# Attention and two gated MLPs on one core: later scores from float32r parts, scaled first-batch queries, eight dummy matmuls

## The chip, the core and the metric

The kernel runs on one core of a Trainium2 chip. The metric is the device time of one execution in microseconds; a time given for a kernel is the median of its runs. TensorE (PE in the rows) multiplies and has a separate weight load (PEld); VectorE (DVE), ScalarE (ACT) and GpSimd (POOL) work elementwise; SyncE (SP) issues the DMAs.

## The reference

Attention with a threshold, then two gated MLPs on its output, all in float32:

```python
scores = scale * q @ k.T                       # 4 batches, 8 heads, 576 x 576, 64 wide
thresh = max(scores) - tau
attn   = softmax(where(scores >= thresh, scores, -1e9))
x      = attn @ v                              # -> 2304 tokens x 512
x      = x / rms(x) * g
x      = (silu(x @ wg) * (x @ wv)) @ wo        # 512 -> 1536 -> 512
x      = (silu(x @ wg2) * (x @ wv2)) @ wo2     # the same once more, no norm
```

The tolerance forbids plain bfloat16, so a float32 product is either done by float32 matmuls or from two float32r parts: a rounded copy (high) and the rest (low), with three products high·high, high·low, low·high.

## The kernel before

The 2304 tokens are worked in three blocks of 768 columns (b = 0, 1, 2). A block's attention covers one full batch and a third, or two parts of batches (`PHASES`); it is cut into 48 tiles of 128 query rows, 144 in all. The first block's 48 tiles are done ahead of everything by `fast`; the 96 later tiles are done by `tile_ops`, strewn between the MLP matmuls of the block before.

A tile's scores go through `QK` (TensorE, two halves of 288 keys in the two banks of a PSUM tile), `MAX` (VectorE, negated row maximum), `THR` (VectorE, threshold and exponent bias from the maximum and tau), `EXP` (ScalarE), `MASK` (VectorE, compare, multiply, sum), `REC` (two small GpSimd or VectorE operations and a reciprocal) and `normalise` (any of three engines, by `NORM_E`). In `fast` the result is transposed on TensorE (line 545, 550), copied out of PSUM (line 590 or 592, by `EV_E`) and multiplied by the values (line 566). In `tile_ops` it is split in two float16 parts (`HI_E`, `LO_E`: lines 461 to 470), transposed by DMA (line 475) and multiplied by the values in parts (lines 661, 664).

Queries and keys lie twice in SBUF, on partitions 0 to 63 and 64 to 127. So `QK` is, for each half j, a float32 matmul on 64 rows, on its own half of the array:

```python
k = slice(64 * j, 64 * j + 64)
nc.tensor.matmul(o[:, j], x[k, c0:c0 + w], x[k, S + j * HS:S + (j + 1) * HS], start=True, stop=True)
```

Of the 96 later tiles 88 hold rows of one head, 8 hold 64 rows of each of two heads, so there are 104 head parts with two such matmuls each. The profile records every float32 matmul as two.

The MLP matmuls are float32r on the whole array, 384 columns at a time (`dense`, line 876; in the last block most gate and value products are done with seven block products in place of eight, `gate_val7`, line 908). After 12 units of gate and value (f = 0 to 11) the output product is made in three pieces (`outp(0)`, `outp(1)`, `outp(2)`, after f = 4, 8 and 11), each from four hidden pieces h. A hidden piece is tanh on ScalarE (line 973), two VectorE operations (974, 985), a rounding copy on ScalarE (992) and a subtraction on VectorE or GpSimd (995); five of them have room (`r_h`).

The order on every engine is made by a planner (`Program.order`): each operation has an engine, an estimated cost, what it depends on and a priority (`OFF`, `OFFF`, the due times `ST` and `SU`), and of what is ready by the estimates the one of least priority goes next. Sets such as `V_E`, `W_E`, `H_E` say which operations go to VectorE and which to GpSimd. The engines then work strictly in that order and wait on semaphores.

Of the kernel before, what the change touches and what calls it, by code (L numbers as in the profile page):

```python
# [35 lines left out]
NU = 18  # L36
NTC = 12
# [58 lines left out]
S_E = (2, 0, 0)
RAWN, TN = 4, 1
ARENA = 17376
PLAIN = 1
GV = [m * NU + i for m in range(2) for i in [0, 1, 2, 3, 4, 7, 8, 9, 10, 13, 14, 15][PLAIN:]]  # L100
A_E = {3, 5, 8, 9, 10, 12, 13, 14, 15, 16, 17, 18, 20, 21, 22, 24, 26, 28, 29, 31, 32, 33, 35}
T_E = {0, 2, 3}

UP, FP, T0, DRAIN, ATT, LEAD, LEAD2, UL, RMS0, RMS1, CREL = 10071, 3560, 170023, -9692, 10886, 14, 9, 8063, -113807, -68190, 73599
OFF = {'MAX': 1748, 'EXP': 56850, 'THR': -2265, 'MASK': -95785, 'REC': 54966, 'NORM': 8371, 'HI': -109767, 'LO': 41933, 'LOL': 2327, 'DT': -94697, 'PV': 24084, 'PVO': 20003, 'PVA': 43347, 'SQ': -155048, 'SQA': -18773, 'SPV': 36844, 'CV': 57404, 'WL': -63278, 'WS2': -7942, 'WS': 9794, 'G': 22245, 'V': 3410, 'HH': 7267, 'YY': 23129, 'PUT': -4270}
OFFF = {'LV': 151718, 'QK': 353, 'MAX': 77575, 'THR': -110770, 'EXP': 9162, 'MASK': 33268, 'REC': -130346, 'NORM': 158475, 'TR': -48808, 'EV': -17099, 'PV': -54831, 'PVO': -31233, 'SQ': 1324, 'SQA': -215375}
EV_E = {0, 35, 5, 37, 8, 9, 41, 12, 46, 15, 49, 19, 51, 23, 27}
XO_E = {8, 17, 6}
# [121 lines left out]
BEGIN = dict(POOL=1400, DMA=1100)  # L230
# [11 lines left out]
def body(ctx: ExitStack, tc: tile.TileContext, qkv, tau, w1, rg, w2, outT):  # L242
# [43 lines left out]
    small = sb.tile([P, 30], F32, name="small")  # L286
# [16 lines left out]

    AR = sb.tile([P, ARENA], F32, name="arena", tag="arena")
# [7 lines left out]
    r_raw = Ring([take(2 * S) for _ in range(RAWN)])  # L312
# [12 lines left out]
    r_h = ring("h", 5, [P, 2, TW], F32R)  # L325
# [7 lines left out]
    late = []  # L333

    def arena2():
        if not late:
            late.append(sb.tile([P, ARENA], F32R, name="arena2", tag="arena"))
        return late[0]

    def TS(a, k):  # L340
        o = (4 * a + k) * 2 * HT
        return arena2()[:, o:o + 2 * HT].rearrange("p (i s) -> p i s", i=2)

    r_s = Ring([lambda i=i: arena2()[:, 16 * HT + i * 3584:16 * HT + (i + 1) * 3584].rearrange("p (a c) -> p a c", a=2) for i in range(3)])
# [4 lines left out]
    def retire():  # L349
        ops = {pg.wrote[k] for k in ("SQ",)} | {i for r in [r_raw, r_v, r_v3, r_e, r_ep, r_e16, r_ag, *r_tmp] for b in r.slots for i in b.ops}  # L350
# [33 lines left out]
    vs, raw = {}, {}  # L384
# [7 lines left out]
    def load(hd):  # L392
        _, c, b, q0, nq, _, _ = PAIRS[hd // 2]
        h = 2 * c + hd % 2
        t = r_raw.next()
# [198 lines left out]
    def tile_ops(n):  # L594
# [17 lines left out]
        for hd, *_ in parts:  # L612
            r += [("rawq", hd), ("rawk", hd)]
# [269 lines left out]
    def moe(b, between):  # L883
        for m in range(2):
# [146 lines left out]
            for f in range(NF):  # L1031
# [11 lines left out]
                elif f == 8:  # L1043
                    outp(1)
# [93 lines left out]
```

## Time and profile before

| | us |
|---|---|
| median of 3 runs | 1191.06 (1191.04 to 1192.66) |
| the profiled execution | 1193.02 |
| its span, first to last instruction | 1191.2 |
| TensorE busy in it | 1160.5 |
| VectorE, ScalarE, GpSimd busy | 840.1, 664.7, 513.2 |

TensorE's busy time counts the way of a matmul through the array, which overlaps the next one; so what a matmul costs in a row of them is read from the distance of their starts. In rows of the timeline the first number is a start, the second runs from the first start to the last end of the merged instructions. The first 18 us of the trace have no record of the granted clock, and the view of windows shows them as 1.00.

### The profile page before, as it was taken

The page shows a single profiled execution, that of the slowest core. Times are in us where ns is not written, and L with a number is a line of the kernel's source. Part 1 is how long each engine was busy: PE and PEld are TensorE (multiplying, and loading weights), DVE is VectorE, ACT ScalarE, POOL GpSimd, SP SyncE. Part 2 cuts the span into 40 slices and gives each one's busy share as a digit, 9 for nine tenths or more (in the row PEclk, how much of TensorE's full clock was granted, in tenths as well). Part 3 has the DMA queues.
Part 4 walks back from the last instruction along what each step waited for, and adds up shares of the span by engine and source line. Part 5 has one row for each costly group of instructions (what it writes and reads, how often), then busy time and mean ns, then how long its engine had stood idle before and what let it go on. Part 6 is the DMA issues. An engine that isn't in the chain of part 4 may idle for free.

```text
span 1191.2 us, 18894 instructions
## 1 busy us (share of the span) xinstructions
PE 1160.5 (97%) x7120; PEld 1024.6 (86%) x7120; DVE 840.1 (71%) x1533; ACT 664.7 (56%) x933; POOL 513.2 (43%) x582
## 2 busy tenths in 40 slices
PE   7998999999999999999999999999999999999998
PEld 4665888888888888888887888888999999999898
DVE  7998776778877777667667676755464867887743
ACT  5779867877887877434444343433332553454421
POOL 1222035656476566483635645432551512352221
PEclk9999989999999999999999999999999999999999
DMA  7323658998897998866683635444334212122111
GB/s 224 99 88 117 243 180 244 277 275 249 247 283 227 261 300 253 271 201 162 167 192 98 156 103 154 104 125 117 137 126 141 72 57 86 54 71 68 57 37 53
DMA packets 175291, 189.85 MB, mean 159 GB/s; under 512 B 143968, under 2 KB 147552, under 8 KB 164960
## 3 DMA queue, kind: packets, MB, share of 16 engines
q1 hardware_dynamic: 175200, 188.65, 54.5%
q8 instruction: 56, 0.92, 0.3%
q14 instruction: 35, 0.29, 0.1%
HBM read 119.93 MB, written 40.37 MB: 135 GB/s over the span
## 4 chain that ended last, share of the span: by engine, by line
PE 86%; DVE 6%; ACT 3%; DMA 2%; issue 1%; POOL 0%; SPq 0%; DVEq 0%; ACTq 0%
PE ps L876 58%; PE pb L908 10%; PE ps L609 5%; PE pt L661 4%; PE ps L908 2%; PE pt L664 2%; PE ps L506 2%; PE pt L566 1%; PE pt L545 1%; DMA arena<-arena 1%; ACT arena L592 1%; DMA arena<-in_qkv 1%; DVE h L995 1%; DMA w<-in_w 1%; DVE col L519 0%
## 5 line engine op out<-in xcount | busy, mean ns | idle before, releaser
L876 PE MATMUL ps<-XS,w 128*128 128x384 f32 x2400 | 445.3, 342 | 4.2 <-DVE th L974 3.0
L876 PEld LDWEIGHTS ps<-XS,w 128*128 128x128 f32 x2400 | 415.2, 190 | 33.7 <-issue 26.6
L876 PE MATMUL ps<-h,w 128*128 128x384 f32 x1728 | 319.0, 340 | 0.9 <-DVE h L995 0.6
L876 PEld LDWEIGHTS ps<-h,w 128*128 128x128 f32 x1728 | 300.1, 188 | 15.6 <-issue 13.0
L995 POOL TENSOR_TENSOR h<-th,h 128x768 fp32r<-128x768 f32 x37 | 71.8, 1941 | 138.6 <-ACT h L992 135.8
L626 DVE TENSOR_REDUCE col<-ps 128x1 f32<-128x576 f32 x96 | 72.3, 753 | 65.4 <-PE ps L609 65.1
L629 DVE SCALAR_TENSOR_TENSOR arena<-ps,col,arena 128x576 f32<-128x576 f32 x96 | 78.1, 814 | 43.4 <-ACT arena L628 42.9
L628 ACT ACTIVATE arena<-ps,col 128x576 f32<-128x576 f32 x96 | 70.9, 738 | 64.3 <-DVE col L627 55.9
L908 PE MATMUL pb<-arena 128*128 128x384 f32 x528 | 102.1, 339 | 3.1 <-DVE X L916 2.9
L908 PEld LDWEIGHTS pb<-arena 128*128 128x128 f32 x528 | 93.7, 191 | 3.8 <-DVE X L916 3.2
L775 ACT CAST w<-w 128x1024 fp32r<-128x1024 f32 x61 | 64.0, 1049 | 51.3 <-PE ps L876 43.2
L777 POOL TENSOR_TENSOR w<-w,w 128x1024 fp32r<-128x1024 f32 x27 | 65.8, 2437 | 52.7 <-ACT w L775 52.6
L992 ACT CAST h<-th 128x768 fp32r<-128x768 f32 x72 | 60.0, 833 | 46.7 <-DVE th L985 23.5
L1024 DVE SCALAR_TENSOR_TENSOR Y<-ps,Y 128x768 f32<-128x768 f32 x48 | 45.7, 954 | 47.3 <-PE ps L876 47.2
L973 ACT ACTIVATE th<-ps 128x768 f32<-128x768 f32 x48 | 38.9, 810 | 68.7 <-PE ps L876 67.2
L609 PE MATMUL ps<-arena 64*128 64x288 f32 (+1 forms) x416 | 73.4, 457 | 2.3 <-DVE arena L629 2.3
L469 POOL TENSOR_TENSOR arena<-arena 128x512 f16<-128x512 f32 x60 | 73.9, 1232 | 0.0
L974 DVE SCALAR_TENSOR_TENSOR th<-th,ps 128x768 f32<-128x768 f32 x48 | 45.6, 949 | 32.9 <-ACT th L973 32.6
L985 DVE SCALAR_TENSOR_TENSOR th<-th,ps 128x768 f32<-128x768 f32 x48 | 45.7, 951 | 32.7 <-PE ps L876 32.5
L450 ACT ACTIVATE arena<-arena,col 128x576 f32<-128x576 f32 x60 | 51.7, 864 | 22.6 <-DVE col L639 20.7
L918 ACT COPY X<-pb 128x384 f32<-128x384 f32 x66 | 31.3, 476 | 56.9 <-PE pb L908 56.7
L816 DVE SCALAR_TENSOR_TENSOR w<-w,t 128x1024 uint32<-128x1024 uint32 x36 | 50.0, 1388 | 7.7 <-ACT t L815 7.4
(146 smaller groups left out, 1781.9 us busy)
## 6 DMA issues: line engine op xcount, KB each, us to landing
w<-in_w SPq DMA_DIRECT2D x36, 1024.0 KB, 6.3
w<-kept SPq DMA_DIRECT2D x25, 1024.0 KB, 5.2
w<-kept SPq DMA_DIRECT2D x47, 512.0 KB, 3.7
kept<-w SPq DMA_DIRECT2D x19, 1024.0 KB, 5.4
kept<-w SPq DMA_DIRECT2D x30, 512.0 KB, 4.3
arena<-in_qkv SPq DMA_DIRECT2D x15, 576.0 KB, 4.3
arena<-in_qkv SPq DMA_DIRECT2D x41, 160.0 KB, 2.7
arena<-in_qkv SPq DMA_DIRECT2D x16, 288.0 KB, 3.3
```

Of the source, the lines that this page charges most:

```text
L450: op("ACT", 760, lambda: nc.scalar.activation(e, e, AF.Identity, bias=c[:, 4:5], scale=c[:, 3:4]), **k)
L469: op(en, 601 if eng == 2 else 1128, lambda: n1.tensor_tensor(h[:, 640:], e[:, :512], h[:, :512], ALU.subtract), lock=True, w=[("lo", n)], ...
L609: nc.tensor.matmul(o[:, j], x[k, c0:c0 + w], x[k, S + j * HS:S + (j + 1) * HS], start=True, stop=True)
L626: op("DVE", 670, lambda: nc.vector.tensor_reduce(c[:, 0:1], s2, AX.XY, ALU.max, negate=True), w=[*sk, ("mx", n)], bufs=[cb], p=T + F['MAX' ...
L628: op("ACT", 640, lambda: nc.scalar.activation(e2, s2, AF.Exp, bias=c[:, 2:3], scale=SCALE), r=[("thr", n)], w=[*sk, ("e", n)] + ek, bufs=[ ...
L629: op("DVE", 822, lambda: nc.vector.scalar_tensor_tensor(e2, s2, c[:, 1:2], e2, ALU.is_ge, ALU.mult, accum_out=c[:, 6:7]), r=[("thr", n)], ...
L775: op("ACT", 939, lambda: nc.scalar.copy(ws[:, 0], w), r=[("w32", n)], w=[("wh", n)], bufs=[b32, sbf], p=p, name=f"w_split{n}")
L777: op(en, 1142 if en == "DVE" else 2340, lambda: n1.tensor_tensor(ws[:, 1], w, f32(ws[:, 0]), ALU.subtract), lock=True, r=[("w32", n), ("wh ...
L876: nc.tensor.matmul(pt[:, j, :HT], w(i, a), x(i, b_)[:, j * HT:(j + 1) * HT], start=(i == 0 and a == 0 and b_ == 0), stop=(i == n - 1 and a ...
L908: nc.tensor.matmul(bank(), w()[:, a, col * 256 + i * P:][:, :P], xf(i, b_), start=first and i == 0 and a == 0 and b_ == 0, stop=i == 1 and ...
L992: op("ACT", 734, lambda: nc.scalar.copy(h[:, 0], tb.t), r=[("th", n)], w=[("h0", n)], bufs=[tb, hb], p=p + OFF['HH'], name=f"h{n}")
L995: op(eng, 878 if eng == "DVE" else 1795, lambda: n1.tensor_tensor(h[:, 1], tb.t, f32(h[:, 0]), ALU.subtract), lock=True, r=[("th", n), ("h ...
```

## The change

- **Scores of the 96 later tiles.** `split` makes, for each head of a later block, a tile of 128 rows: the rounded queries (64 rows) over the rest of the queries (64 rows), the rounded keys twice, and the rest of the keys twice. The rounding copies are ScalarE's or GpSimd's, the subtractions VectorE's or GpSimd's, by the new set `Q_E`. `QK` is then four float32r matmuls on 128 rows and 288 columns per head part, two that add up in each bank. A tile of two heads adds them up over eight, with columns of zeros for the other head's rows.
- **First block.** The queries are multiplied by 1/8 as they come in (one ScalarE and 16 GpSimd operations). The exponential takes the negated maximum itself as bias; `THR` is a GpSimd operation that only the mask waits for.
- **Start.** Eight float32 128x128x128 matmuls on the identity stand first on TensorE; the loads of tau and of the norm's weights are issued from ScalarE's queue in place of SyncE's.
- **Room.** The raw queries and keys get tiles of their own (five slots in the first block, two after it, with two for the parts); the arena is smaller; four hidden pieces have room in place of five, and `outp(0)` and `outp(1)` come after f = 3 and 7. The weights stand in DRAM as before and are read in the new order (`ROW`).
- **Tables.** Priorities, planner costs and all sets are new. In the first block 8 normalisations are VectorE's (16 before), 20 GpSimd's (8), 20 ScalarE's (24); VectorE has 16 copies of 512 columns (9), 9 of 128 (5), and 7 of the output copies (3). 36 weight pieces are kept with 16 stores of 1 MB and 26 of 0.5 MB (19 and 30).

```diff
-    r_raw = Ring([take(2 * S) for _ in range(RAWN)])
+    RA, RX = sb.tile([P, 4 * S], F32, name="ra", tag="ra"), sb.tile([P, 2 * XW], F32, name="rx", tag="rx")
+    slots = [RA[:, i * 2 * S:(i + 1) * 2 * S] for i in range(2)] + [RX[:, i * 2 * S:(i + 1) * 2 * S] for i in range(3)]
+    r_raw, r_raw2 = Ring(slots), Ring(slots[:2])
+    r_x = Ring([lambda i=i: again("rx", 2 * XW)[:, i * XW:(i + 1) * XW] for i in range(2)])
...
-    r_h = ring("h", 5, [P, 2, TW], F32R)
+    r_h = ring("h", 4, [P, 2, TW], F32R)
...
+            if hd == 0 and c0 == 0:
+                op("ACT", 180, lambda q=q: nc.scalar.activation(q, q, AF.Copy, scale=SCALE), w=keys, bufs=[tq], p=T_ - 20000, name=f"scale{hd}")
+            else:
+                op("POOL", 190 + (z - c0) * 8 // 10, lambda q=q: nc.gpsimd.tensor_scalar(q, q, SCALE, 1.0, ALU.mult, ALU.mult), w=keys, bufs=[tq], p=T_ + OFFF['QS'], name=f"scale{hd}")
...
+        for i, (key, a, z, o) in enumerate((("q", q0, q0 + nq, column(hd, q0)), ("k", S, 2 * S, S + 64))):
+            if 4 * hd + i in Q_E:
+                op("POOL", ..., lambda o=o, a=a, z=z: nc.gpsimd.tensor_scalar(xs()[:, o:o + z - a], ys[:, a:z], 1.0, 1.0, ALU.mult, ALU.mult), ...)
+            else:
+                op("ACT", ..., lambda o=o, a=a, z=z: nc.scalar.copy(xs()[:, o:o + z - a], ys[:, a:z]), ...)
+            en, n1 = ("DVE", nc.vector) if 4 * hd + 2 + i in Q_E else ("POOL", nc.gpsimd)
+            if i:
+                op(en, c, lambda n1=n1: n1.tensor_tensor(xs()[:, 2 * S + 64:], ys[:, S:], f32(xs()[:, S + 64:2 * S + 64]), ALU.subtract), ...)
+            else:
+                op(en, c, lambda n1=n1, o=o, a=a, z=z: n1.tensor_tensor(xs()[64:, o:o + z - a], ys[64:, a:z], f32(xs()[64:, o:o + z - a]), ALU.subtract), ...)
...
-            op("DVE", 130, lambda c=c, s=s: nc.vector.scalar_tensor_tensor(c[:, 1:3], s[:, 1, KC:KC + 2], c[:, 0:1], K2, ALU.mult, ALU.add), r=[("mx", n), "tau"], w=[("thr", n), *sk], ...)
-            op("ACT", 640, lambda c=c, s2=s2, e2=e2: nc.scalar.activation(e2, s2, AF.Exp, bias=c[:, 2:3], scale=SCALE), r=[("thr", n)], ...)
+            op("POOL", 270, lambda c=c: nc.gpsimd.tensor_scalar(c[:, 1:2], c[:, 0:1], K0[:, 0:1], ntau, ALU.mult, ALU.add), r=[("mx", n), "tau"], w=[("thr", n)], ...)
+            op("ACT", 640, lambda c=c, s2=s2, e2=e2: nc.scalar.activation(e2, s2, AF.Exp, bias=c[:, 0:1]), r=[("mx", n)], ...)
...
         def QK():
-            for hd, c0, w, m in parts:
-                x = raw[hd].t
-                o = s[m:m + w, :, :HS]
-                for j in range(2):
-                    k = slice(64 * j, 64 * j + 64)
-                    nc.tensor.matmul(o[:, j], x[k, c0:c0 + w], x[k, S + j * HS:S + (j + 1) * HS], start=True, stop=True)
+            for j in range(2):
+                for u, (hd, c0, w, m) in enumerate(heads):
+                    x = parts[hd].t()
+                    c = column(hd, c0) - m
+                    for i in range(2):
+                        k = S + 64 + (2 * i + j) * HS
+                        nc.tensor.matmul(s[:, j, :HS], x[:, c:c + P], x[:, k:k + HS], start=i + u == 0, stop=i == 1 and u == len(heads) - 1)
...
-                if f == 4:
+                if f == 3:
                     outp(0)
-                elif f == 8:
+                elif f == 7:
                     outp(1)
...
+    op("PE", 213 * WARM, warm, w=["PC"], p=-1e9, name="warm", cols=512 * WARM)
+    op("ACT", 60, lambda: nc.scalar.dma_start(taus, tau), w=["tau0"], p=-1e9, name="tau")
```

TensorE in the first MLP, at the end of the last gate and value unit ahead of `outp(0)`; `w` are weights, `XS` the inputs, `h` the hidden pieces, `ps_70` the scores' PSUM tile. Before:

```order
L876 MATMUL ps_65<-XS,w_103 128x384 x6
L609 MATMUL ps_70<-arena 128x288 x2
L876 MATMUL ps_65<-XS,w_103 128x384 x18
L876 MATMUL ps_66<-h_89,w_104 128x384 x6
L876 MATMUL ps_66<-h_90,w_104 128x384 x6
L876 MATMUL ps_66<-h_91,w_104 128x384 x6
L609 MATMUL ps_70<-arena 128x288 x2
L876 MATMUL ps_66<-h_92,w_104 128x384 x6
```

The same place after:

```order
L925 MATMUL ps_65<-XS,w_103 128x384 x18
L661 MATMUL ps_70<-rx_1190 128x288 x4
L925 MATMUL ps_65<-XS,w_103 128x384 x6
L925 MATMUL ps_66<-h_91,w_104 128x384 x6
L925 MATMUL ps_66<-h_92,w_104 128x384 x6
L925 MATMUL ps_66<-h_93,w_104 128x384 x6
L661 MATMUL ps_70<-rx_1190 128x288 x4
L925 MATMUL ps_65<-h_91,w_104 128x384 x6
L925 MATMUL ps_66<-h_94,w_104 128x384 x6
```

Each pair of matmuls of the scores has become four, at about the same places. The fourth hidden piece (`h_92` before, `h_94` after) is now that of the unit just ended, and another six matmuls on an older piece stand ahead of it.

VectorE at the start, from the third maximum on; `ps_65`, `ps_66`, `ps_70` are the three tiles of scores. Before:

```order
L520 SCALAR_TENSOR_TENSOR col<-ps_70,col,small 128x2
L520 SCALAR_TENSOR_TENSOR col<-ps_66,col,small 128x2
L519 TENSOR_REDUCE col<-ps_65 128x1
L522 SCALAR_TENSOR_TENSOR Y,col<-ps_70,col,Y 128x576
L520 SCALAR_TENSOR_TENSOR col<-ps_65,col,small 128x2
```

After:

```order
L573 SCALAR_TENSOR_TENSOR Y,col<-ps_70,col,Y 128x576
L570 TENSOR_REDUCE col<-ps_65 128x1
L573 SCALAR_TENSOR_TENSOR arena,col<-ps_66,col,arena 128x576
L570 TENSOR_REDUCE col<-ps_70 128x1
L573 SCALAR_TENSOR_TENSOR Y,col<-ps_65,col,Y 128x576
```

The thresholds (L520) are gone from VectorE, and masks and maxima alternate.

GpSimd after its constants (there is nothing between the constants and the first `REC` before), after the change:

```order
L1098 TENSOR_SCALAR small<-small 128x1
L1099 TENSOR_SCALAR small<-small 128x1
L431 TENSOR_SCALAR ra<-ra 128x448
L431 TENSOR_SCALAR ra<-ra 128x576
L431 TENSOR_SCALAR rx<-rx 128x192
L571 TENSOR_SCALAR col<-col,small 128x1
```

The first threshold (L571) stands behind the scaling of the queries of the second and of the third head (L431), which wait for their loads.

## Rows read from the trace of the kernel before

**Rows 1.** Windows by stage: us; busy of PE, PEld, DVE, ACT, POOL; PEclk; DMA; GB/s.

```profile
20.00:100.00 80.00, 75.62 (x750) 49.71 (x749) 74.69 (x199) 64.40 (x126) 19.14 (x55) 1.00 0.33 97
...
165.00:500.00 335.00, 334.31 (x1895) 286.38 (x1895) 251.42 (x423) 259.76 (x305) 205.48 (x252) 1.00 0.91 262
500.00:850.00 350.00, 347.26 (x2097) 301.89 (x2096) 224.11 (x496) 140.68 (x211) 165.97 (x179) 1.00 0.55 143
850.00:1191.20 341.20, 332.92 (x1905) 330.68 (x1903) 227.07 (x299) 137.26 (x195) 112.87 (x65) 0.99 0.24 81
```

**Rows 2.** Waits of TensorE: for whom, us in total, times, longest us.

```profile
PE ps L609 <- DVE arena L629: 2.3, 1, 2.3
PE pt L661 <- DMA arena<-arena: 1.1, 2, 0.7
...
PE ps L876 <- DVE h L995: 0.6, 1, 0.6
```

**Rows 3.** Timeline of TensorE around one later tile's scores (L609).

```profile
362.57 4.33 PE L876 MATMUL ps<-XS,w 128*128 128x384 f32 x24
366.82 0.76 PE L609 MATMUL ps<-arena 64*128 64x288 f32 x4
367.51 2.18 PE L876 MATMUL ps<-XS,w 128*128 128x384 f32 x11
```

**Rows 4.** The chain in order of time: start, us, what; float32r matmuls without a break.

```profile
966.34 6.24 PE pb L908 x36
```

**Rows 5.** The same timeline around a tile of two heads.

```profile
581.25 0.72 PE L609 MATMUL ps<-arena 64*64 64x288 f32 x8
581.90 1.32 PE L876 MATMUL ps<-h,w 128*128 128x384 f32 x6
```

**Rows 6.** The page's groups: count | busy us, mean ns | idle before it, releaser.

```profile
L609 PE MATMUL ps<-arena 64*128 64x288 f32 (+1 forms) x416 | 73.4, 457 | 2.3 <-DVE arena L629 2.3
```

**Rows 7.** Timeline of weight loads around the scores of rows 3.

```profile
366.39 0.19 PEld L876 LDWEIGHTS ps<-XS,w 128*128 128x128 f32 x1
...
367.51 0.30 PEld L876 LDWEIGHTS ps<-XS,w 128*128 128x128 f32 x2 [0.39 <-issue]
```

**Rows 8.** Groups by shape on VectorE, 0 to 117 us.

```profile
L520 DVE SCALAR_TENSOR_TENSOR col<-ps,col,small 128x2 f32<-128x2 f32 x48 | 9.8, 214 | 0.4
L590 DVE COPY arena<-pt 128x512 f32<-128x512 f32 x9 | 6.2, 684 | 1.1 <-PE pt L545 1.1
L448 DVE TENSOR_SCALAR arena<-arena,col 128x576 f32<-128x576 f32 x8 | 4.6, 574 | 0.0
...
L590 DVE COPY arena<-pt 128x128 f32<-128x128 f32 x5 | 1.4, 279 | 0.0
```

**Rows 9.** Groups by shape on GpSimd, 0 to 117 us.

```profile
L527 POOL TENSOR_SCALAR col<-col 128x2 f32<-128x2 f32 x20 | 4.8, 238 | 60.1 <-DVE Y L522 29.8 <-DVE arena L522 29.3 <-DVE col L531 1.0
...
L446 POOL TENSOR_SCALAR arena<-arena,col 128x576 f32<-128x576 f32 x4 | 3.3, 823 | 3.4 <-DVE col L520 1.4 <-PE ps L508 1.2 <-DVE col L531 0.8
```

**Rows 10.** Timeline of the start: the first mask, transposes on TensorE.

```profile
9.29 0.81 DVE L522 SCALAR_TENSOR_TENSOR Y<-ps,col,Y 128x576 f32<-128x576 f32 x1
...
14.13 1.97 PE L545 MATMUL pt<-ident,Y 128*128 128x128 f32 x8 [0.71 <-DVE Y L448]
```

**Rows 11.** Timeline of TensorE: transposes later in the first stage.

```profile
19.39 0.66 PE L545 MATMUL pt<-ident,arena 128*128 128x128 f32 x4
```

**Rows 12.** Groups by shape, whole span: work like the new splitting, and a hidden piece's last steps.

```profile
L469 POOL TENSOR_TENSOR arena<-arena 128x512 f16<-128x512 f32 x60 | 73.9, 1232 | 0.0
...
L995 POOL TENSOR_TENSOR h<-th,h 128x768 fp32r<-128x768 f32 x37 | 71.8, 1941 | 138.6 <-ACT h L992 135.8 <-DVE col L626 2.9
...
L992 ACT CAST h<-th 128x768 fp32r<-128x768 f32 x72 | 60.0, 833 | 46.7 <-DVE th L985 23.5 <-DVE th L942 23.0
...
L469 DVE TENSOR_TENSOR arena<-arena 128x512 f16<-128x512 f32 x36 | 24.9, 692 | 0.0
...
L461 ACT CAST arena<-arena 128x576 f16<-128x576 f32 x32 | 21.4, 667 | 19.7 <-DVE arena L448 15.7 <-issue 2.2 <-POOL X L677 1.7
```

More of the change, by code (lines that the diff above doesn't have):

```diff
@@ L96 @@
 S_E = (2, 0, 0)
-RAWN, TN = 4, 1
-ARENA = 17376
+TN = 1
+XW = 3 * S + 64
+WARM = 8
+ARENA = 12768
 PLAIN = 1
[L100 to L105, printed above, removed]
@@ L229 @@
 TICK = 10240 / 3
-BEGIN = dict(POOL=1400, DMA=1100)
+BEGIN = dict(POOL=1400, DMA=1100, PE=1500)
 LAT = {
@@ L285, in body @@
     make_identity(nc, ident)
-    small = sb.tile([P, 30], F32, name="small")
+    small = sb.tile([P, 31], F32, name="small")
+    ntau = small[:, 30:31]
     ones = small[:, 18:20]
@@ L302, in body, with again @@
     SS = RB = sb.tile([P, TW], F32, name="SS")
+    late = {}
+    def again(tag, n):
+        if tag not in late:
+            late[tag] = sb.tile([P, n], F32R, name=tag + "2", tag=tag)
+        return late[tag]
     AR = sb.tile([P, ARENA], F32, name="arena", tag="arena")
@@ L332, in body @@
     r_w = ring("w", 3, [P, 2, 1024], F32R)
[L333 to L338, printed above, removed]
     def TS(a, k):
-        o = (4 * a + k) * 2 * HT
-        return arena2()[:, o:o + 2 * HT].rearrange("p (i s) -> p i s", i=2)
-    r_s = Ring([lambda i=i: arena2()[:, 16 * HT + i * 3584:16 * HT + (i + 1) * 3584].rearrange("p (a c) -> p a c", a=2) for i in range(3)])
+        i, w = 4 * a + k, 2 * HT
+        t, o = (again("rx", 2 * XW), i) if i < 4 else (again("ra", 4 * S), i - 4) if i < 7 else (again("arena", ARENA)[:, 3 * 3584:], 0)
+        return t[:, o * w:(o + 1) * w].rearrange("p (i s) -> p i s", i=2)
+    r_s = Ring([lambda i=i: again("arena", ARENA)[:, i * 3584:(i + 1) * 3584].rearrange("p (a c) -> p a c", a=2) for i in range(3)])
     r_u = Ring([X.rearrange("p c s -> p (c s)")[:, i * 3 * HT:(i + 1) * 3 * HT].rearrange("p (u s) -> p u s", u=3) for i in range(2)])
@@ L382, in SK @@
         return [("SS", k) for k in range(a // 64, z // 64)]
-    vs, raw = {}, {}
+    vs, raw, parts, scales = {}, {}, {}, []
     def T_head(hd):
@@ L394, in load @@
         h = 2 * c + hd % 2
-        t = r_raw.next()
+        if hd == 2 * NFG:
+            for i in range(2):
+                r_raw2.slots[i].ops = list(r_raw.slots[i].ops)
+                r_x.slots[i].ops = [o for sl in r_raw.slots[2:] for o in sl.ops]
+        t = (r_raw if hd < 2 * NFG else r_raw2).next()
         raw[hd] = t
@@ L892, in gate_val7 @@
                 wb = wsp[n]
-                (b1, k1), (b2, k2), (b3, k3) = SETS[(next(x for x in (4, 8, 11) if x >= f) - f) % 2]
+                (b1, k1), (b2, k2), (b3, k3) = SETS[(next(x for x in (3, 7, 11) if x >= f) - f) % 2]
                 ub = r_u.next()
@@ L1040, in moe, with tau_consts, warm @@
                     tiles(2 * NTB)
[L1041 removed]
+                if f == 3:
                     outp(0)
[L1043 removed]
+                elif f == 7:
                     outp(1)
             outp(2)
[L1048 to L1049 removed]
+    def tau_consts():
+        nc.gpsimd.tensor_scalar(ntau, taus, -1.0, 1.0, ALU.mult, ALU.mult)
+        nc.gpsimd.tensor_scalar(K2[:, 0:1], taus, -1.0 / SCALE, 1.0, ALU.mult, ALU.mult)
+    def warm():
+        for _ in range(WARM):
+            nc.tensor.matmul(PC[:, :P], ident, ident, start=True, stop=True)
+    op("PE", 213 * WARM, warm, w=["PC"], p=-1e9, name="warm", cols=512 * WARM)
+    op("ACT", 60, lambda: nc.scalar.dma_start(taus, tau), w=["tau0"], p=-1e9, name="tau")
+    op("POOL", 130, lambda: tau_consts(), r=["tau0"], w=["tau"], rel=4000.0, p=-1e9, name="tau")
     for t, key in ((PA, "PA1"), (PB, "PB1"), (PD, "PD1")):
         op("ACT", 200, lambda t=t: nc.scalar.copy(t[:, 1, KC:KC + 2], K0), w=[key], p=0, name="K1")
[L1052 removed]
+    op("ACT", 60, lambda: nc.scalar.dma_start(rgs, rg), w=["rg"], p=-1e9, name="rg")
     done = [0]
```

90 lines of the change are left out of this document (59 added, 31 removed).

## The prediction

> **What bounds the kernel now.** I read the windows by stage first [rows 1]. From 165 us to the end TensorE is busy for 334.3 of 335, 347.3 of 350 and 332.9 of 341 us, while VectorE, ScalarE and GpSimd hold 60 to 78% in the densest of these stretches (251.4, 259.8 and 205.5 of 335). Then TensorE's waits [rows 2]: the longest behind 165 us are single ones of 2.3 us or less. So from 165 us on the time is TensorE's own work, and a matmul taken out there comes off the end, as long as the others keep up. Between 20 and 100 us it is otherwise: TensorE 75.6 and VectorE 74.7 of 80, ScalarE 64.4; no one engine sets the pace alone, and what one loses another may hold. Last I read starts on TensorE around the scores, since its busy time doesn't say what a group costs.
>
> **Scores of the later tiles, the large term.** A float32r matmul of 384 columns in an unbroken row takes 6.24/36 = 0.1733 us [rows 4]. In [rows 3] 24 such start at 362.57, so a 25th would start at 366.73; the scores start at 366.82, 0.09 later. The next MLP matmul starts at 367.51, 0.69 after the scores. Of the 11 that follow, the last ends at 369.69; with an end 0.34 us after its own start it starts at 369.35, 1.84 behind the first, where ten steps are 1.73: so 0.11 is lost once more. One tile of one head costs 0.09 + 0.69 + 0.11 = 0.89 us. A tile of two heads [rows 5] costs 0.65 from start to start; behind it six matmuls' last start is 0.98 after the first, where five steps are 0.87, 0.11 lost; with the same 0.09 ahead it is 0.85. The 416 records [rows 6] are 88 tiles at 4 and 8 at 8.
>
> After, a tile of one head is four float32r matmuls of 288 columns on the whole array, a tile of two heads eight. The trace has that type at 384 columns alone. At the granted clock (level 2.4 GHz, share 1.00 there) 384 columns stream in 0.160, so 0.0133 is added; for 288 I take 0.120 + 0.0133 = 0.133 us. The ends are 0.120 (nothing added) and 0.173 (no shorter than at 384). The weights have to be there in time: behind the scores, where nothing is loaded ahead, two loads take 0.30 together, where one takes 0.19 [rows 7], so they follow each other at 0.11, under the 0.120 of the stream. And I take no loss at the borders, since before and after stand matmuls of the same type and the same 128x128 tile, between which [rows 4] none shows. So 4 x 0.133 = 0.53 and 8 x 0.133 = 1.07 us. **Sum: 88 x (0.89 - 0.53) = 31.7 off, 8 x (1.07 - 0.85) = 1.8 on, 29.9 us off.** Ends: with 0.120, 88 x 0.41 = 36.1 off less 8 x 0.11 = 0.9, 35 off; with 0.173, 88 x 0.20 = 17.6 off, 8 x 0.53 = 4.3 on, 13 off.
>
> A rule of the Trainium skill speaks against this. Before, two 64-row matmuls run side by side on two halves of the array and the change gives that up. "TensorE: Matmul & The Clock Gate", Part 3, says moreover that a weight load overlaps a running matmul only where the row groups differ, and they don't between whole-array matmuls. By that rule [rows 4] would read 0.160 + 0.11 and more for each; it reads 0.173, so the trace doesn't agree where matmul follows matmul.
>
> **The splitting that pays for it.** 32 head loads each need two rounding copies and two subtractions: 48 copies on ScalarE, 16 on GpSimd, 25 subtractions on VectorE, 39 on GpSimd. By like rows [rows 12] a copy of 576 is 0.67 us on ScalarE, a subtraction of 512 is 0.69 on VectorE, 1.23 on GpSimd: at most 32 us on ScalarE, some 17 on VectorE, some 45 on GpSimd, all between about 120 and 870 us. From 165 to 500 the cover is what [rows 1] leaves free of 335 us, 84 on VectorE, 75 on ScalarE, 130 on GpSimd; half of the splitting fits in. What it can cost is order: a score's matmuls in front of the MLP's wait if the parts are late, and all of TensorE's queue behind them. I put 4 us, from 0 to 14 (14 is about half of the gain).
>
> **outp one unit sooner.** The fourth hidden piece must now be ready right after its own unit, at 12 more places (`outp(0)` and `outp(1)`, two MLPs, three blocks). Before, this holds at `outp(2)`, six places, and all waits for h by VectorE add up to 0.6 us [rows 2]: 0.1 each, 1 us for 12. The matmuls on older pieces that stand ahead, 24 x 0.173 = 4.2 us, cover copy and subtraction, 0.83 + 1.94 [rows 12]. If GpSimd is busy when the copy ends, another 1.94 isn't covered: 12 x 1.94 = 23 is the upper end, and 0 the lower.
>
> **The first stage.** VectorE loses 48 thresholds, 9.8 us, and 8 normalisations at 0.574, 4.6; it gains 7 copies at 0.684 and 8 small ones at about 0.28, 7.0 [rows 8]: 7.4 us less. ScalarE loses those copies and 4 normalisations. GpSimd gains 48 thresholds at about 0.24, 12 normalisations at 0.82 [rows 9], and the scaling, 16 operations between its small and its 576-column price: 11 + 10 + 4 to 13 on 19.1 of 80 us [rows 1], hidden. All 7.4 us come off only if VectorE alone sets the pace; TensorE, unchanged, has 4.4 of 80 us free, 5 on the whole stage. I take 4 off, from 0 to 8.
>
> **The start.** The first mask begins at 9.29 [rows 10]. The new exponential doesn't wait for tau, but the mask's threshold stands on GpSimd behind the scaling of the second and third head, whose loads come about then: no gain there. Eight transposes take 1.97 us at 14 us, four take 0.66 at 19 [rows 10, 11], so TensorE is slow up to there; eight dummies ahead of the first loads may end that sooner. 1 us off, from 1 on (first scores queue behind the dummies) to 2 off. The stretch from 100 to 165 us and the stores (5 MB fewer) I leave at nothing; 3 either way for the first.
>
> **Sum.** 1193.0 (the profiled execution; span 1191.2 and 1.8 around it) - 29.9 + 4 + 1 - 4 - 1 = 1163.1. The median lies 2.0 under that execution, so I predict **1161 us**.
>
> **Rivals**, all on the median.
> - *The others set the pace.* ScalarE and VectorE, three quarters full, and DMA (share 0.91 from 165 to 500) can't follow TensorE, and half of the gain stands as new waits: 15 back, 1176. For it: that stretch; against it: 0.7 us of DMA waits there at a time [rows 2], and only 55% DMA from 500 on.
> - *288 columns cost as 384.* The step is set by something other than the stream: 13 off instead of 30, 1178. Against it: the added 0.0133 is small beside the stream.
> - *Hidden pieces late.* 23 in place of 1 for outp: 1183.
> - *Loads not hidden, slower.* If two loads don't run under the shorter streams, a matmul takes 0.120 + 0.013 + 0.11 = 0.243, a tile 0.97 or 1.94: 88 x 0.08 + 8 x 1.09 = 16 on instead of 30 off, 1207. It decides above (88 x 0.89 + 8 x 0.85)/416 = 0.204 us a matmul. Against it stands [rows 4]; for it that 0.120 leaves but 0.01 over 0.11.
>
> **How the numbers follow.** Forecast 0.64 (its own range 1150 to 1170), others set the pace 0.17, as 384 columns 0.07, pieces late 0.05, loads not hidden 0.04; 0.03 for a new order that by several waits in TensorE's queue eats all the gain. The range goes from 1148 (35 off, first stage 8 off, and some of the 4 and 1 left) to 1180, which takes in the first two rivals. Faster by over 0.2% (2.4 us, about what a measurement here can tell from none) 0.91, within it 0.03, slower 0.06.
>
> **What would show it.** In the trace after: groups of four matmuls of scores about 0.53 from start to start of the next, with 0.173 straight ahead and behind; 0.24 would be the slower rival. TensorE without waits over 2 us from 165 us on, its instructions ending some 30 us sooner between 165 and 870; waits on the splitting's lines (471 to 479) or on h would show rivals one and three. The first stage's last maximum some 4 us sooner. A gain that lies mostly ahead of 165 us, or a loss behind 870, would make my reading wrong.

## The result and the profile after

The changed kernel took 1173.7 us (median of 4, 1172.6 to 1180.9), the kernel before beside it 1191.9 (1191.0 to 1196.4): a ratio of 0.985, interval 0.981 to 0.990. Two more sets of five runs gave 1172.9 (ratio 0.985, 0.982 to 0.987) and 1172.8 (0.984, 0.982 to 0.987). So it is faster by 18 to 21 us, inside the predicted 1148 to 1180, with about two thirds of the 30 forecast. The profiled executions tell the same: 1193.0 before, 1172.7 after, 20.3 less.

The page of the changed kernel: span, busy time of each engine, and the group of the later scores (busy, mean ns | idle before, releaser); they answer to the table of before and to [rows 6].

```profile
span 1170.9 us, 19172 instructions
...
PE 1138.1 (97%) x7136; PEld 1058.4 (90%) x7136; DVE 874.5 (75%) x1559; ACT 689.2 (59%) x973; POOL 588.3 (50%) x663
...
L661 PE MATMUL ps<-rx 128*128 128x288 f32 x416 | 71.9, 297 | 3.0 <-DVE arena L678 2.9
```

The windows of the changed kernel, columns as in [rows 1]:

```profile
20.00:100.00 80.00, 74.34 (x735) 48.45 (x729) 71.03 (x167) 55.58 (x107) 43.88 (x109) 1.00 0.30 92
...
165.00:500.00 335.00, 330.39 (x1954) 308.18 (x1953) 266.56 (x452) 271.00 (x332) 238.56 (x279) 1.00 0.89 250
500.00:850.00 350.00, 347.02 (x2165) 329.49 (x2164) 268.85 (x566) 167.50 (x247) 169.31 (x158) 1.00 0.56 143
850.00:1170.90 320.90, 313.92 (x1786) 312.94 (x1784) 203.03 (x267) 127.72 (x185) 108.90 (x59) 0.99 0.23 79
```

TensorE still fills the time from 165 us on, but no longer as tightly: 4.6 us idle from 165 to 500 in place of 0.7. The scores' group counts the same 416 records with nearly the same busy time as in [rows 6], 71.9 against 73.4: busy time shows nothing of the gain. The distances of the starts do. The timeline of TensorE after, around a tile of one head (L661 are scores, L925 MLP matmuls, L710 and L713 value products):

```profile
445.78 2.76 PE L925 MATMUL ps<-XS,w 128*128 128x384 f32 x15
448.38 0.69 PE L661 MATMUL ps<-rx 128*128 128x288 f32 x4
448.90 1.20 PE L925 MATMUL ps<-XS,w 128*128 128x384 f32 x6
452.38 1.62 PE L710 MATMUL pt<-arena 128*128 128x384 f16 x9 [2.27 <-DMA arena<-arena]
...
648.44 0.80 PE L661 MATMUL ps<-rx 128*128 128x288 f32 x4
649.09 4.33 PE L925 MATMUL ps<-XS,w 128*128 128x384 f32 x24
653.25 1.22 PE L661 MATMUL ps<-rx 128*128 128x288 f32 x8
654.31 4.33 PE L925 MATMUL ps<-XS,w 128*128 128x384 f32 x24
```

Fifteen steps of 0.1733 are 2.60, and the scores start 2.60 after the first: nothing is lost ahead. From there to the next MLP matmul it is 0.52 for four, 0.13 each; eight take 1.06. A tile of one head in [rows 3] cost 0.89. The group at 648.44 takes 0.65: it stands right behind a value product (L713), and there the first of the four takes 0.24 to the next one. The fourth row shows the other side, a new wait: the value product stood 2.27 us for its transposed parts.

The waits of TensorE between 165 and 850 us, columns as in [rows 2]:

```profile
PE pt L710 <- DMA arena<-arena: 3.4, 3, 2.3
PE ps L661 <- DVE arena L678: 2.9, 4, 1.4
PE ps L925 <- DVE th L1023: 0.7, 1, 0.7
```

To see where the 20.3 us went I count MLP matmuls (both kernels issue them in nearly the same order) and compare the start of the same one:

| stretch | before, us | after, us | difference | made of |
|---|---|---|---|---|
| start to first MLP matmul | 118.8 | 118.7 | -0.1 | |
| first to 200th | 51.3 | 52.4 | +1.1 | scores -1.7, rest +2.7 |
| 200th to 3250th | 694.9 | 675.7 | -19.2 | scores -26.1, waits +5.7, twelve matmuls of a later norm +1.3 |
| 3250th to the end | 326.3 | 324.2 | -2.1 | those twelve -1.3, waits -0.9 |

The scores' part is their own starts plus what the MLP matmuls beside them lost. This is one execution of each kernel. In two further profiles of the changed kernel (below) the stretches are 54.5 and 53.6, 673.1 and 675.2, 324.1 and 322.8 us: the large one holds within 3 us. TensorE's idle time from the 200th to the 3250th, 3.4 us before, is 7.6, 4.2 and 6.9 in the three. Up to 1.5 us of the -19.2 is the clock: from 639.6 to 643.0 us the kernel before ran at a granted clock of 0.50 (1.2 GHz), the changed one, in its first profile, nowhere in that stretch.

### The profile page after: what moved, and what is told of

Same layout as the page of the kernel before. It is cut to its first block, busy times and chain, and to the rows that moved or that the text cites. A ratio compares the mean times of both kernels' runs of the same rounds, so it can differ in the third digit from the quotient of the medians.

```text
span 1170.9 us, 19172 instructions
## 1 busy us (share of the span) xinstructions
PE 1138.1 (97%) x7136; PEld 1058.4 (90%) x7136; DVE 874.5 (75%) x1559; ACT 689.2 (59%) x973; POOL 588.3 (50%) x663
## 4 chain that ended last, share of the span: by engine, by line
PE 81%; DVE 6%; DMA 4%; ACT 4%; issue 2%; POOL 2%; SPq 0%; POOLq 0%; DVEq 0%; ACTq 0%
PE ps L925 53%; PE pb L957 12%; PE ps L661 4%; PE pt L710 4%; DMA arena<-arena 2%; PE ps L957 2%; DMA arena<-in_qkv 2%; PE pt L713 2%; PE pt L617 1%; PE ps L557 1%; PE pt L596 1%; ACT arena L643 1%; DVE w L865 1%; DVE col L570 1%; DVE Y L573 1%
## 5 line engine op out<-in xcount | busy, mean ns | idle before, releaser
L925 PE MATMUL ps<-XS,w 128*128 128x384 f32 x2400 | 438.9, 339 | 4.4 <-DVE XS L814 2.4
L925 PEld LDWEIGHTS ps<-XS,w 128*128 128x128 f32 x2400 | 415.4, 189 | 11.5 <-issue 4.3
L925 PE MATMUL ps<-h,w 128*128 128x384 f32 x1728 | 318.4, 338 | 2.8 <-DVE Y L1073 2.8
L925 PEld LDWEIGHTS ps<-h,w 128*128 128x128 f32 x1728 | 302.6, 188 | 6.0 <-DVE Y L1073 3.7
L1044 POOL TENSOR_TENSOR h<-th,h 128x768 fp32r<-128x768 f32 x33 | 64.5, 1955 | 103.3 <-ACT h L1041 103.3
L826 POOL TENSOR_TENSOR w<-w,w 128x1024 fp32r<-128x1024 f32 x30 | 74.4, 2480 | 83.2 <-ACT w L824 83.1
L957 PE MATMUL pb<-rx,arena 128*128 128x384 f32 x352 | 100.0, 338 | 0.0
L824 ACT CAST w<-w 128x1024 fp32r<-128x1024 f32 x60 | 62.9, 1049 | 44.6 <-PE ps L925 32.1
L661 PE MATMUL ps<-rx 128*128 128x288 f32 x416 | 71.9, 297 | 3.0 <-DVE arena L678 2.9
L661 PEld LDWEIGHTS ps<-rx 128*128 128x128 f32 x416 | 63.4, 188 | 7.0 <-DVE arena L678 4.6
L895 POOL TENSOR_TENSOR arena<-w,arena 128x768 fp32r<-128x768 f32 (+1 forms) x20 | 47.1, 2376 | 41.8 <-ACT arena L894 41.7
L957 PEld LDWEIGHTS pb<-rx,arena 128*128 128x128 f32 x352 | 64.5, 188 | 0.0
L1023 DVE SCALAR_TENSOR_TENSOR th<-th,ps 128x768 f32<-128x768 f32 x48 | 45.6, 950 | 22.3 <-ACT th L1022 22.0
L520 POOL TENSOR_TENSOR arena<-arena 128x512 f16<-128x512 f32 x52 | 61.2, 1178 | 0.0
```

The source lines that it names most:

```text
L520: op(en, 601 if eng == 2 else 1128, lambda: n1.tensor_tensor(h[:, 640:], e[:, :512], h[:, :512], ALU.subtract), lock=True, w=[("lo", n)], ...
L661: nc.tensor.matmul(s[:, j, :HS], x[:, c:c + P], x[:, k:k + HS], start=i + u == 0, stop=i == 1 and u == len(heads) - 1)
L824: op("ACT", 939, lambda: nc.scalar.copy(ws[:, 0], w), r=[("w32", n)], w=[("wh", n)], bufs=[b32, sbf], p=p, name=f"w_split{n}")
L826: op(en, 1142 if en == "DVE" else 2340, lambda: n1.tensor_tensor(ws[:, 1], w, f32(ws[:, 0]), ALU.subtract), lock=True, r=[("w32", n), ("wh ...
L925: nc.tensor.matmul(pt[:, j, :HT], w(i, a), x(i, b_)[:, j * HT:(j + 1) * HT], start=(i == 0 and a == 0 and b_ == 0), stop=(i == n - 1 and a ...
L957: nc.tensor.matmul(bank(), w()[:, a, col * 256 + i * P:][:, :P], xf(i, b_), start=first and i == 0 and a == 0 and b_ == 0, stop=i == 1 and ...
```

## Experiments

Ratios are to the kernel before on the same chip, from five rounds each. First the whole again, and what the largest part is worth by itself.

**The changed kernel again**, twice:

> The changed kernel once more, as the measure for the others of this call. Both theories: between 1172.6 and 1174.7 us, as in the first runs.

> The kernel after the change once more, as the measure for the two others of this call: 1172.8 us within 1.5, the first normalisation at 140 to 143 us.

Measured: 1172.9 and 1172.8. In their profiles the 200th MLP matmul starts at 173.8 and 173.0 (171.0 in the first one): a profile's single events move by 2 to 3 us between executions, the medians of the three sets by 0.9. Much of it is TensorE's clock: from 150 to 160 us the granted clock is 0.66 in these two and 0.83 in the first, so they spend more of it at the lower level (1.2 GHz). What that costs shows in the first profile: twelve MLP matmuls took 4.04 us at 132.4 us, mostly at the lower level, and 2.35 at 126.1, at the full clock.

**Scores by float32 again:**

```
- for each head part and half j: two float32r matmuls, 128 rows, x 288 columns
+ for each head part and half j: one float32 matmul on its 64 rows; split() not called; five raw slots
```

> The changed kernel with the later scores by float32 matmuls on 64 rows again, no splitting, all five raw slots used throughout; the planner orders it anew by the same tables. Theory 1 (the scores' matmuls give their whole 28 us, and what is missing of the forecast was lost elsewhere): slower than the changed kernel by 24 to 30 us, so 1197 to 1204, and slower than the kernel before; in the trace the later scores cost 0.89 us a tile again, and the first MLP matmul starts at 118 to 119 us as in both. Theory 2 (VectorE, ScalarE and GpSimd, loaded with the splitting, take back a part of the gain): slower by 10 to 20 us only, 1184 to 1194.

Measured: 1203.5 (1203.2 to 1205.7), ratio 1.011 (1.008 to 1.013): 30.6 above the changed kernel. Its timeline around a tile (L639 scores, L903 MLP matmuls) has the old pattern back:

```profile
379.66 2.28 PE L903 MATMUL ps<-h,w 128*128 128x384 f32 x12
381.88 0.76 PE L639 MATMUL ps<-ra 64*128 64x288 f32 x4
382.56 4.51 PE L903 MATMUL ps<-h,w 128*128 128x384 f32 x24
```

Scores at 2.22 where twelve steps are 2.08, and 0.68 to the next. By the starts some 27 of the 30.6 us are the scores' own; the rest is waits in this order (from the first to the 200th MLP matmul it takes 58.1 us, 3.6 of them idle ahead of scores). So this part carries the whole gain; the rest of the change is worth nothing, or less: this kernel is 11.5 us slower than the one before. How much of that comes from tables made for other costs stays open.

**What splitting costs:**

```
- n1.tensor_tensor(low, raw, high, subtract)   # both, for queries and for keys
+ (not issued; the scores' second halves read the high keys again)
```

> The changed kernel with the 64 subtractions of the splitting planned but not issued (25 on VectorE, 39 on GpSimd); the scores read the high parts in their place, so their values are not the reference's. Everything else stands in the same order. Theory 1: faster than the changed kernel by 3 to 6 us, about 1168, with TensorE's waits ahead of the scores and of the value matmuls between 165 and 870 us gone by half. Theory 2: faster by 8 us or more.

Measured: 1170.8 (1169.2 to 1174.7), 2.1 under the changed kernel measured beside it (1170.8 to 1175.7), less than either expected and hardly clear of the scatter: the ratios' intervals, 0.981 to 0.986 and 0.982 to 0.987, overlap. TensorE's waits ahead of scores and value products between the 200th and the 3250th MLP matmul sum to 2.6 us; in the three profiles of the changed kernel they are 6.5, 3.1 and 5.9, so that half of them went is not shown.

**The dummies:**

```
- for _ in range(WARM):
+ for _ in range(0):
```

> The changed kernel with the eight dummy matmuls planned but not issued. Theory 1 (they matter little, since TensorE falls back to the lower clock at 10.5 us): within 1 us of the changed kernel, 1172 to 1175; the first maximum 0 to 0.2 us sooner. Rival (the early clock counts): 1 to 3 us slower, with the first MLP matmul as much later.

Measured: 1172.7 (1170.6 to 1174.4): no difference. The timelines of TensorE show why, first with the dummies (L1103; L557 scores, L596 transposes), then without; between them two windows with the dummies, columns as in [rows 1]:

```profile
1.35 3.78 PE L1103 MATMUL pt<-ident 128*128 128x128 f32 x16 [1.35 <-POOL ident masks.py:199]
5.06 2.39 PE L557 MATMUL ps<-ra 64*128 64x288 f32 x8
...
8.51 0.76 PE L557 MATMUL ps<-ra 64*128 64x288 f32 x4 [1.06 <-POOL ra L431]
...
15.61 1.90 PE L596 MATMUL pt<-ident,Y 128*128 128x128 f32 x8
```

```profile
10.00:15.00 5.00, 4.23 (x16) 1.82 (x16) 4.97 (x12) 2.76 (x4) 2.67 (x9) 0.55 1.04 391
15.00:20.00 5.00, 4.98 (x43) 3.33 (x39) 4.89 (x13) 3.78 (x6) 2.80 (x7) 0.77 0.85 252
```

```profile
11.65 1.33 PE L557 MATMUL ps<-ra 64*128 64x288 f32 x4
...
15.85 1.85 PE L596 MATMUL pt<-ident,Y 128*128 128x128 f32 x8
```

With them the first scores start at 5.06 (4.43 without, 3.83 before), and eight transposes at 15.6 are as slow as ever (1.97 in [rows 10]). The dummies did reach the clock, for a moment: four records of scores take 0.76 us at 8.5 us where they take 1.33 without, and this trace's record of the granted clock reads 1.00 from 7.1 to 10.5 us. Then TensorE waited (1.06 us ahead of 8.51, 0.75 ahead of 10.02), and from 10.5 to 17.3 us the granted clock is 0.50 (1.2 GHz). In the second profile of the changed kernel four records take 1.33 us throughout: there the dummies did nothing.

Then the first stage, which I had at 4 us and which gave nothing. First theories: ScalarE's queue sets its end (theory 1), or VectorE's.

**Thresholds back on VectorE:**

```
- op("POOL", 270, ... nc.gpsimd.tensor_scalar(...))   # THR of the first block
+ op("POOL", 270, ... nc.vector.tensor_scalar(...))   # same place in the order
```

> The first block's 48 thresholds are issued by VectorE (as before the change) instead of GpSimd, at the same place in the order. Theory 1: the end of the first stage is set by ScalarE's queue (exponentials with the first weight units' conversions among them), so the first MLP matmul stays at 118.7 us within 1 and the total at 1172.9 within 1.5. Rival: VectorE's queue sets the pace of the first stage; then 48 instructions of 0.15 to 0.21 us each come back and the first MLP matmul and the total are 7 to 10 us later.

Measured: 1172.9 (1170.3 to 1176.2), no difference; the first MLP matmul at 120.1, 0.8 to 1.5 later than in the changed kernel's profiles. VectorE doesn't set the pace: 48 instructions, 12.7 us of its time in this trace, move the end by about 1.

**Conversions left out.** ScalarE is busy 18.0 of the 18 us from 100 to 118 in both kernels, with the first weight units' conversions among the exponentials.

```
- lambda: nc.scalar.activation(q, top, ...)               # three per unit
+ lambda: None if n < 2 else nc.scalar.activation(q, top, ...)
```

> The kernel before with ScalarE's conversions of the first two weight units not issued (the weights are wrong for it), which takes 7.4 us off ScalarE's queue around 97 to 121 us; all else in the same order. Theory 1: ScalarE's queue sets the end of the first stage, so the first MLP matmul, at 118.8 us before, comes 3 to 7 us sooner. Rival: the end is set by GpSimd or VectorE, or by the weights' transfers; then it moves by less than 1 us.

> The kernel after the change with ScalarE's conversions of the first two weight units not issued (the weights are wrong for it); all else in the same order. Theory 1: the first MLP matmul, at 118.7 us in after, comes 4 to 9 us sooner, and some 2 us sooner than in the kernel before with the same conversions left out: the scores of the first stage ended 2.2 us sooner in after, and ScalarE's queue had taken that back. Rival: it moves by less than 1 us, or both kernels move alike.

Measured: before 1189.8 (ratio 0.9986, 0.9969 to 1.0004), after 1172.6: neither moves by more than the runs can tell. The first MLP matmul came 1.4 us sooner in before (117.4) and 1.9 in after (116.8), out of 7.4 us taken away. Theory 1 as I put it falls, and what else holds the first MLP matmul at 118.7 in both kernels stays open. What was won was gone again by the 100th MLP matmul: 151.4 without the conversions, 151.6 with.

**A collision between 118 and 128 us.** The timelines of VectorE and GpSimd after (L826 is a weight's subtraction, L635 a sum of squares, L477 and L479 the first split):

```profile
122.62 1.53 DVE L477 TENSOR_TENSOR rx<-ra,rx 128x576 fp32r<-128x576 f32 x1
124.08 2.40 DVE L635 TENSOR_TENSOR SS<-SS,arena 128x64 f32<-128x64 f32 x1
...
122.03 1.50 POOL L479 TENSOR_TENSOR rx<-ra,rx 64x384 fp32r<-64x384 f32 x1 [5.36 <-ACT X L643]
123.97 2.42 POOL L826 TENSOR_TENSOR w<-w,w 128x1024 fp32r<-128x1024 f32 x1 [0.43 <-ACT w L824]
```

A sum of 64 columns takes 2.40 us beside GpSimd's subtraction; elsewhere 0.22. The Trainium skill ("SBUF — State Buffer", "Who interferes with whom") states that a VectorE instruction with two inputs in SBUF contends with a GpSimd instruction that reads SBUF; this pair agrees. Is it the cause?

```
- n1.tensor_tensor(...)                                      # rests of unit 1 and of the first pair's queries
+ (nc.vector if n == 1 else n1).tensor_tensor(...)           # likewise for the queries
```

> Between 118 and 150 us GpSimd works beside VectorE, and VectorE's small instructions there take 1.5 to 2.4 us where 0.2 to 0.3 are usual. Here weight unit 1's rests and the first pair's query rests are made by VectorE instead of GpSimd, at the same place in the order. Theory 1: the two engines collide there and that delays the first sum of squares; without it the 50th to 200th MLP matmul start 2 to 4 us sooner than after's, and the total is 1 to 3 us shorter than 1172.9. Rival: the long instructions there don't hold up the chain; the same milestones within 1 us and the total within 1 us, or later, as VectorE has more to do.

Measured: 1174.5 (1171.1 to 1179.7), none of the milestones sooner. The 64-column sum takes 0.22 again, and nothing comes of it.

**Transfers.** The first normalisation (L771, L722 before) started at 140.3 to 142.5 us in the changed kernel's profiles, at 139.0 before. In before, four raw loads went out between 100 and 110 us; in after they stand behind the second weight load, at 123.6 to 127.9, in full DMA engines.

```
- nc.sync.dma_start(t.t[:, c0:c1], qkv[b, h, :, c0:c1])
+ None if hd in (2 * NFG + 2, 2 * NFG + 3) else nc.sync.dma_start(...)   # first kernel
+ op("DMA", ..., rel=142000 if hd in (...) else 0)                       # second: not before then in the plan
```

> The four raw loads of the second later pair (queries and keys of two heads, 0.98 MB, issued at 123.6 to 127.9 us in after, where the DMA engines are busy 0.92 to 1.01 of the time from 120 to 140 us; in before they were issued between 100 and 110 us, at a DMA share of 0.39) are not issued, so that pair's scores come from the first pair's data and part of the output is not the reference's. All else is in the same order. Theory 3: full DMA engines hold VectorE's queue (its combination of the values waits for their load, and the first normalisation stands behind it), and these loads add 2.5 to 3 us there. Then the value load is 2 to 3 us sooner, the first normalisation starts at 137.5 to 139.5 us (140.1 to 143.1 in every run of the changed kernel with these loads there, 139.0 and 139.2 in the two of the kernel before), and the total is 1 to 3 us under after's of the same call. Rival: the queues of VectorE and ScalarE are full for other reasons, and the normalisation starts at 140 to 143 us all the same.

> The same four loads are released later, so that they stand in SyncE's queue behind the next weight load (issued at 138.4 us in after) and not ahead of two; on the other engines nothing moves but one pair of VectorE's instructions that changes places. Nothing is left out. Theory 3: as without those loads, the first normalisation starts at 137.5 to 139.5 us, and the total is 1 to 3 us under after's, since the second pair's scores are needed only after 160 us; this would then be the better kernel. Rival: it starts at 140 to 143 us as before, and the total is after's within 1 us, or above it by a wait of the second pair's scores for the later loads.

Measured: 1172.6 and 1173.5, the normalisation at 140.3 and 141.6. DMA's busy share from 125 to 130 us fell from 1.00 to 0.50 and 0.54. The value load that VectorE waits for landed at 138.8 in the first, as in the changed kernel (138.8 to 141.0), at 137.7 in the second. There the pair that changed places puts a weight's conversion (L865) behind the values' combination, and its subtraction then stands for ScalarE's rounding copy of that weight (L824):

```profile
140.45 1.23 DVE L826 TENSOR_TENSOR w<-w,w 128x1024 fp32r<-128x1024 f32 x1 [1.12 <-ACT w L824]
```

Theory 3 falls, and the second is no better kernel.

**Two brakes at once.** The rows left two: the timeline of VectorE without the conversions (L486 combines a head's values, L826 a weight's subtraction) has the first normalisation right behind a wait for a load,

```profile
138.57 0.49 DVE L486 TENSOR_TENSOR arena<-arena 128x320 f32<-128x320 f32 x1 [2.14 <-DMA arena<-in_qkv]
138.98 1.22 DVE L826 TENSOR_TENSOR w<-w,w 128x1024 fp32r<-128x1024 f32 x1
140.12 4.27 DVE L771 SCALAR_TENSOR_TENSOR X<-X,small,SS 128x768 f32<-128x768 f32 x4
```

while in the changed kernel's first profile the conversion chain ends at the same time: ScalarE's rounding copy (L824) at 139.11, and the combination, begun when the load had landed (138.77), lets the same subtraction start at 139.18. So both have to go:

```
+ conversions of units 0 and 1 not issued, as above, and
- nc.sync.dma_start(v.t[:, :, 0], vp)
+ nc.gpsimd.memset(v.t[:, :, 0], 0.0) if hd == 2 * NFG + 2 else nc.sync.dma_start(v.t[:, :, 0], vp)
```

> The changed kernel without ScalarE's conversions of the first two weight units, and besides without the load of one head's values that VectorE's queue waited for at 138.6 us without the conversions (a fill with zeros on GpSimd stands in its place; weights and those values are wrong for it). Theory 4: the first normalisation has two brakes that end within a microsecond of each other, the conversion chain of weights through ScalarE and VectorE and that load; with both taken off it starts at 138.5 to 139.3 us (140.1 without the conversions alone, 140.3 to 142.5 in the changed kernel, 139.0 in before), the 100th dense matmul starts 1 to 2 us before 151.4, and the total goes down by at most 2 us. Rival: a third brake stands there as well, and the normalisation starts at 140 us or later.

Measured: 1170.0 (1166.6 to 1171.7), ratio 0.982 (0.979 to 0.985), 2.6 under the conversions left out alone. Its timeline:

```profile
136.97 1.23 DVE L826 TENSOR_TENSOR w<-w,w 128x1024 fp32r<-128x1024 f32 x1 [0.71 <-ACT w L824]
138.11 3.80 DVE L771 SCALAR_TENSOR_TENSOR X<-X,small,SS 128x768 f32<-128x768 f32 x4
```

The normalisation starts 2.0 us sooner than with the conversions alone left out, even sooner than I had put it, the 100th MLP matmul 2.5 sooner (148.9) and the 200th 2.7 (168.4). Whether this stays to the end is not shown: the 3250th starts at 845.5 and 845.6 in the two profiles, and the ratios' intervals, 0.979 to 0.985 and 0.981 to 0.986, overlap. For the normalisation theory 4 stands: two brakes end together. With the conversions alone gone the load holds it, as the run shows. That with the load alone gone the conversions would hold it is an estimate from the rows: the subtraction could start at 139.11 in place of 139.18.

## Why the prediction was right, and where it was off

**What bounds the kernel** was read rightly: from 165 us on what came off TensorE came off the end, and float32 scores cost 30.6 us. That no wait behind 165 us was over 2.3 us wasn't: the profile of before has one of 2.9 (L908, for VectorE's L916), behind 850 us, where no scores stand. After, two are over 2 us, 2.27 in the rows above and 2.8 behind 850 us, though I had named their absence as a sign. The others didn't set the pace, which would have cost 15 us in new waits.

**The scores: -29.9 forecast, -27.8 measured** by the starts. The step of 0.133 held (0.13 by the rows above, eight in 1.06 for 1.07), no loss at the borders was right between MLP matmuls, and so the rivals of 384 columns and of loads that aren't hidden are out. The Trainium skill's rule ("TensorE: Matmul & The Clock Gate", Part 3) would have put a weight load between these whole-array matmuls; each has a load of its own, and eight stand at 0.13 us: as in [rows 4] the trace doesn't agree. The missing 2.1 lie at borders with value products: I took one tile that stands between MLP matmuls, 0.89, and multiplied it by 88. By the starts some 20 of the 96 groups before stand next to a value product and had lost less at that border; after, nine stand right behind one and lose 0.11 each, which I had put at nothing.

**Waits from splitting and from outp: +5 forecast, +4.8 measured** from the 200th matmul on (+5.7, then -0.9), but not where I had them, and in one pair of profiles: by the idle times above the two others of the changed kernel have less. The size is right by luck in part. None waits for h, so the term for outp is 0. The splitting's subtractions are some 2 us by the median, within the scatter. The others are a value product's late transposed parts (2.27 at one place) and masks on VectorE that came late (1.4 at one place).

**The first stage and the start: -5 forecast, 0 measured, and +2.7 more behind it.** This is the step that failed, and 7.7 of the 9.6 us between forecast and result (the first to the 200th MLP matmul took 52.4 us in this profile, 54.5 and 53.6 in the two others, 51.3 before). I took VectorE's 7.4 us less, let half of it come off, and called the stretch from 100 to 165 nothing. But the stage's busy times are a mean over 80 us, and its end isn't in them: in the last 18 us ScalarE is full, and from 118 us on TensorE works through raw columns until the first normalised ones are there. That normalisation ends a queue on VectorE that holds the first weights' conversions and the combination of a head's values, whose load comes late. In before, that load went out at 126.3 and was there at 130. In the changed order the first stage's last value product stands behind twelve more MLP matmuls, and on SyncE the load stands behind a store of a weight (L871), which these rows of TensorE, SyncE and VectorE after show with what hangs on it:

```profile
129.58 0.95 PE L617 MATMUL pt<-arena 128*64 128x64 f32 x20 [0.67 <-ACT arena L643]
...
132.00 0.33 SPq L871 DMA_DIRECT2D kept<-w  x1
132.42 0.39 SPq L444 DMA_DIRECT2D arena<-in_qkv  x1
...
138.77 0.49 DVE L486 TENSOR_TENSOR arena<-arena 128x320 f32<-128x320 f32 x1 [0.74 <-DMA arena<-in_qkv]
...
140.31 4.26 DVE L771 SCALAR_TENSOR_TENSOR X<-X,small,SS 128x768 f32<-128x768 f32 x4
```

and the same events before:

```profile
125.33 0.95 PE L566 MATMUL pt<-arena 128*64 128x64 f32 x20
...
126.31 0.38 SPq L418 DMA_DIRECT2D arena<-in_qkv  x1
...
130.06 0.48 DVE L435 TENSOR_TENSOR arena<-arena 128x320 f32<-128x320 f32 x1
...
138.98 3.81 DVE L722 SCALAR_TENSOR_TENSOR X<-X,small,SS 128x768 f32<-128x768 f32 x4 [1.74 <-ACT SS L719]
```

The load goes out 6.1 us later. The value product ends 4.2 us later (130.53 for 126.28); for the other 1.9 SyncE, which issues in order, stood at that store; in before the next store comes behind the load, at 130.16. Then the load lands 6.3 us after its issue, in before 3.5, though the DMA engines are full in both (busy 0.96 and 0.92 from 130 to 140 us after, 1.01 and 0.91 from 125 to 135 before); why it is slower stays open. That the places of the value product and the store cost the normalisation anything is read from the order and not tried. One run speaks against it: without the conversions the load went out 1.8 us sooner (130.6) and landed only 0.2 sooner (138.6). And the order on VectorE has a part: with float32 scores again the normalisation started at 139.1, since there the weight's subtraction of 1.2 us that stands ahead of it (L826 at 139.18) comes behind it. That load and conversions together hold the normalisation is shown by the last experiment.

Of the +2.7 its start accounts for 1.3; the rest is within what single events move between executions. It is hardly the clock: between the first and the 200th MLP matmul both kernels spend 6.8 us at 1.2 GHz in these two profiles.

The last scores of the first block did start sooner, at 105.8 in place of 108.0, about half of what I had named for a sign. It was no good sign: a stage that others wait for has to be judged by the first thing that uses it.

## What to carry to other kernels

Cost a matmul by the distance of starts in its own surroundings, not by busy time, and count how many stand between which neighbours before multiplying. A gain in a stage without one full engine counts only when the next stage's first user comes sooner: follow that user's queue to its front, loads included. Where leaving out one suspect shows nothing, look for a second one that ends at the same time and leave out both.

## What the runs showed of the hardware beyond this

- A VectorE sum of 64 columns took 2.40 us beside a GpSimd subtraction of 1024 columns (2.42), and 0.22 alone.
- Float32r matmuls of 288 columns with a new 128x128 weight each stand 0.13 us apart, those of 384 columns 0.173: 0.04 for 96 columns, which is one column a cycle at the granted clock of 1.00 (2.4 GHz). Right behind a value product the first of them takes 0.24 to the next.
- Eight dummy matmuls from 1.35 to 5.1 us did not end TensorE's slow start for good: in one execution the clock was up from 7.1 to 10.5 us and fell again after waits of 1.06 and 0.75 us, in another it did not rise before 17.5. The granted clock reads 0.55 from 10 to 15 us and 0.77 from 15 to 20 with them, and the transposes at 15.6 take as long without.
